# Two gated long convolutions: the filters' first transforms as 64-row products, and another layout of the accumulation banks

## The chip, the core and the metric

The kernel runs on one core of a Trainium2 chip. The metric is the time of one execution on the device, in microseconds. The kernel before takes 766.85 us (median of three runs, 766.52 to 771.82). Engines are named as in the profile: PE (matrix products, with its weight loads apart as PEld), DVE, ACT, POOL and SP, which issues most transfers.

## What is computed

x of 2048 positions and 512 channels passes through four layers: A, B, A, B, each added to x, each on a layer norm of x.

```python
def _A_ref(q, k, v, shift_k, ssm_k, ssm_D):      # q = layernorm(x)
    k_shift = sum over t < 4 of k_pad[:, t:t + S, :] * shift_k[:, 3 - t]
    kv = k_shift * v
    y = causal_conv_by_fft(kv, ssm_k)             # per channel, length 2048
    return q * (y + kv * ssm_D)

def _B_ref(u, log_A_real, A_imag, C_real, C_imag, log_dt, D_skip):   # u = layernorm(x)
    K = 2 * real(sum over 128 modes of C * dt * exp((-exp(log_A_real) + 1j * A_imag) * dt * pos))
    return causal_conv_by_fft(u, K) + u * D_skip
```

Layer A's convolution doesn't depend on x, so the kernel does it once and uses it twice. B's taps K are worked out from the modes.

## The kernel before, in words

A transform of length 4096 is done in two steps of matrix products. For channels in groups of 32, the first step (`fwd_group`, `fwd_rows`, line 171) multiplies a tile of 128 rows, which are two halves of 64 rows, each by its own weights. In the *whole* form (`full`) the weights `wz[:, a, :]` have 128 rows of which the other half are zeros, and 16 channels at a time give two products of 128x256 that share one PSUM bank. In the *half* form, for 32 channels at a time, each product takes 64 rows only, writes 512 columns, and the two of a pair (a = 1, 0) lie in the two banks of a double bank (`wide_bank`, tag "f1"). Either way two transposes on DVE (lines 191 and 189) bring 32 channels out of PSUM. The second step (`f2_chunk`, line 196) makes a chunk `pu` of four frequencies from all 128 channels of a quarter; a quarter has eight chunks.

PSUM has eight banks. Until the convolution of B begins they are: "c1", three, for everything of layer A (pf, pu, pi, po and acc); "pm", two, for the magnitudes of the tap stream and for the spectra of B; "pa", two, for its angles; "pk", one, for its sums. After that: "c1" four and "f1" two double banks. So the half form is used in the convolution of B alone.

The work until then is two generators, run in turns (`run_steps`: one step of the stream, two of the other):

- The stream (`taps`, lines 544 to 578) makes B's taps in 64 steps: `angles` (line 484: a product into pa, rounding on DVE, a second product into the same bank), `waves` (lines 495 to 497, sines on ACT), `products` (lines 507 to 511, POOL and DVE, the last readers of the bank pa) and `contract` (line 521 into pk). Every eighth step makes twelve `mags` (line 469 into pm, exponentials on ACT, line 475) for the next two groups of 8 channels at once. After each 16 steps a quarter of B's spectrum follows (`spectrum_quarter(1, ...)`, 12 steps, one with each step of the stream).
- The other (`diagonal`) makes the four quarters of A's spectrum (`spectrum_quarter(0, ...)`, 4 + 8 steps each: first transforms of the tile kk, then the chunks pu, which ACT copies into one of two buffers pc and SP writes to DRAM, lines 247 and 248), and in the same steps `gated`: POOL makes four products `term` (line 619), ACT copies the first into a bank `acc` (line 625), DVE adds the others (line 627) and multiplies into `un` (line 629), 16 groups in all. `un` uses the buffers of pc. Row statistics of x are also taken here (line 637). When all this has been issued, the convolution of A follows (lines 270 to 327).

Then come `gated_update` (lines 724 to 743: ut on ACT, x on DVE), the norm, and the convolution of B, whose tiles in SBUF take the place of the stream's. The order of instructions on each engine is the tile framework's, which lists what is ready by the order of the program, on a timeline that it works out when it builds the kernel.

Of the kernel before, what the change touches and what calls it, by code (L numbers as in the profile page):

```python
# [9 lines left out]
F32 = mybir.dt.float32  # L10
# [5 lines left out]
PSUM = bass.MemoryType.PSUM  # L16
# [83 lines left out]
def kernel(ctx: ExitStack, tc: tile.TileContext, out, x_in, kv_in, ssmk_in, ssmd_in,  # L100
                           la_in, ai_in, cr_in, ci_in, ldt_in, ldtb_in, dsk_in,
                           w1_in, w2_in, mm_in, w4_in, minus_in, tt_in, tg1_in, tg2_in, dbg=None):
    nc = tc.nc
    V, S, G, T = nc.vector, nc.scalar, nc.gpsimd, nc.tensor

    def sbuf(stack, name, side="left"):
        return stack.enter_context(tc.tile_pool(name=name, bufs=1, side=side, reuse_waits="tile"))
# [8 lines left out]
    kdram = [dram.tile([128, 512], F32, name=f"kdram{g}") for g in range(16)]  # L116
# [18 lines left out]
    wz = cpool.tile([128, 2, 128], F32, name="wz")  # L135
# [4 lines left out]
    st0 = cpool.tile([128, 16, 6], F32, name="st0")  # L140
    var, rs, nm, nb = [cpool.tile([128, 16], F32, name=n) for n in ("var", "rs", "nm", "nb")]

    psum, w1, swapped = {}, [], [None]

    def bank(name, tag="c1"):
        pool, bufs = psum[tag]
# [13 lines left out]
    def fwd_rows(src, pf, j, step, rows, full):  # L160
        for a in (1, 0):
            half = slice(0, 128) if full else slice(64 * a, 64 * a + 64)
            w = wz[:, a, :] if full else w1[0][half, :]
            rhs = src(half, j, step)[:, rows, :]
            o = pf[:, a].rearrange("p x t r -> p t x r")[:, rows]
            if len(rhs.shape) == 4:
                o = o.rearrange("p t (i x) r -> p t i x r", i=rhs.shape[2])
                rhs = rhs.rearrange("p t i (x r) -> p t i x r", r=2)
            else:
                rhs = rhs.rearrange("p t (x r) -> p t x r", r=2)  # L170
            yield T.matmul(o, w, rhs, start=True, stop=True)  # L171
# [51 lines left out]
    def spectrum_quarter(which, q, src, pool, zlast, zb, tag):  # L223
        z = pool.tile([128, 64, 32, 2], F32, name="zk", tag="z", bufs=zb) if which else z_of_a()
        dr = pool.tile([1, 128], F32, name="dr", tag="dr", bufs=1)
        nc.sync.dma_start(dr, (ssmd_in, dsk_in)[which][:, 128 * q:128 * q + 128])
        for g in range(4):
            kk = pool.tile([128, 512], F32, name="kk", tag="kk", bufs=3 - which)
            nc.sync.dma_start(kk, src[4 * q + g])
            d = dr[:, 32 * g:32 * g + 32]  # L230
            if which == 0:
                kv = kk.rearrange("p (t c) -> p t c", c=32)
                view = lambda ps_, j, n: kv[ps_, :, j:j + n]
            else:
                kv = kk.rearrange("p (i t c) -> p t i c", i=4, c=8)
                view = lambda ps_, j, n: kv[ps_, :, j // 8:(j + n) // 8, :]
                d = d.rearrange("p (i c) -> p i c", c=8)

            G.tensor_add(kv[0:1, 0], kv[0:1, 0], d)  # L239
            fwd_group(view, z, 32 * g, 32, 16, zlast[-zb] if len(zlast) >= zb else None, tag)  # L240
            yield
        for c in range(NCH):
            pu, ins = f2_chunk(z, c, None, tag)
            if c == NCH - 1:
                zlast.append(ins)
            pc = pool.tile([128, CK * 128], F32, name="pc", tag="pc", bufs=2)
            S.copy(pc, pu.rearrange("p k c -> p (k c)"))  # L247
            nc.sync.dma_start(spec[which][q][c], pc)
            yield
# [96 lines left out]
    for a in range(2):  # L346
        half = slice(64 * a, 64 * a + 64)
# [77 lines left out]

    pctx = ExitStack()
    pp = pctx.enter_context(tc.tile_pool(name="ps", bufs=1, space=PSUM, reuse_waits="tile"))
    NPA = 2
    NPM = 2
    psum["c1"] = (pp, 7 - NPA - NPM)  # L430
    psum["pm"] = (pp, NPM)

    for tag, bufs in (("c1", 7 - NPA - NPM), ("pa", NPA), ("pk", 1)):
        pp.tile([128, 512], F32, name=tag, tag=tag, bufs=bufs)
    wk = sbuf(gctx, "wk")
    kp = sbuf(gctx, "spec_k")
    NT = 3
# [26 lines left out]
    def mags(gi, k, col):  # L464
        h, s = divmod(k, 2)
        hs = slice(64 * h, 64 * h + 64)
        pm = pp.tile([128, 512], F32, name="pm", tag="pm", bufs=NPM)
        rhs = tabs["tg2"][hs] if col == 2 else tabs["tg1"][hs, 8 * s:8 * s + 8, :]
        mt = T.matmul(pm, rows[gi][hs, 1, :], rhs, start=True, stop=True)  # L469
        if col == 2:  # L470
            ms[gi, h] = wk.tile([128, 16, 96], F32, name="m", tag="m", bufs=NM)
            m = ms[gi, h][:, :, 64:96]
        else:
            m = ms[gi, h][:, 8 * s:8 * s + 8, 0:64]
        i = S.activation(m, pm.rearrange("p (c i) -> p c i", c=16 if col == 2 else 8), AF.Exp)  # L475
        if last_sin[0] is not None:
            after(i, last_sin[0])
        last_exp[0] = i
# [58 lines left out]
    zlast_k, todo = [], []  # L537
# [6 lines left out]
    def taps():  # L544
        load_rows(0)
        load_rows(1)

        def exps(gi):
            for k in range(4):
                if k % 2 == 0:  # L550
                    mags(gi, k, 2)
                mags(gi, k, 1)

        for n in range(64 + LP + LC):
            gi, k = divmod(n, 4)
            if n < 64:
                if k == 0:
                    if gi > 0 and gi < 15:
                        load_rows(gi + 1)
                    if EORD == 1:  # L560
                        exps(gi)
                    elif EORD == 3 and gi % 2 == 0:
                        exps(gi)
                        exps(gi + 1)
                if n == XN:
                    root = normalizer(0, 16, lambda t: st0[:, t, :])
                    after(root, last_exp[0])
                    last_exp[0] = root
                angles(gi, k)
                waves(gi, k)  # L570
            if 0 <= n - LP < 64:
                products(*divmod(n - LP, 4))
            m = n - LP - LC
            if 0 <= m < 64:
                contract(*divmod(m, 4))
                if m % 16 == 15:
                    todo.append(spectrum_quarter(1, m // 16, kdram, kp, zlast_k, 1, "pm"))
            yield

    def stream():  # L580
# [20 lines left out]
    with ExitStack() as actx:  # L601
        ap = sbuf(actx, "conv_a", "right")
        zlast = []
        ZA = 2
# [38 lines left out]
        def steps_a(q):  # L643
            z, us = {}, {}
            nop = lambda: None

            def load(g):
                us[g] = ap.tile([128, 16, 32], F32, name="u", tag="kk", bufs=3)
                nc.sync.dma_start(us[g].rearrange("p t c -> p (t c)"), kv_d[4 * q + g])

            def fwd(g):
                if g == 0:
                    z[0] = z_of_a()
                u = us[g]
                fwd_group(lambda ps_, j, n: u[ps_, :, j:j + n], z[0], 32 * g, 32, 16, zlast[4 + q - ZA])
                if g < 3:
                    load(g + 1)
            turns = [lambda g=g: fwd(g) for g in range(4)]
            if LAGA > 2:
                turns = [nop, turns[0], turns[1], lambda: (turns_last[0](), turns_last[1]())]  # L660
                turns_last = [lambda: fwd(2), lambda: fwd(3)]
            return (lambda: z[0]), [nop] * 7 + [lambda: load(0)] + [nop] * 4 + turns
# [6 lines left out]
        def diagonal():  # L669
# [17 lines left out]
                    yield  # L687
            for _ in kvs:
                yield
            yield from convolution(0, {"conv": ap}, steps_a, finish_a, lag=LAGA, ahead=AHA, nk=NKA, ns=NSA, nw=NWA, inplace=True,  # L690
                                   add_dve=ADA, zlast=zlast)

        RT = 1
        RD = 2
        diag = diagonal()
        for _ in range(4):
            next(diag)
# [2 lines left out]

    xp = sbuf(ctx, "xp", "right")
    st = xp.tile([128, 16, 4, 6], F32, name="st")
    w1.append(xp.tile([128, 128], F32, name="w1"))
    nc.sync.dma_start(w1[0], w1_in)
    st_all = lambda t: st[:, t, :, :].rearrange("p q s -> p (q s)")

    def gated_update(buffer, spare, rnd, load_x=False):
# [49 lines left out]
    EF = 1  # L757
# [25 lines left out]
    def steps_b(rnd, q):  # L783
        z = {}
        u = rotating("u", [128, 16, 128], "u", 3)
# [26 lines left out]
        early = {}  # L812
# [12 lines left out]
        def fwd(c):  # L825
            if c == 0:
                z[0] = rotating("zu", [128, 64, 32, 2], "zu", 2)
            if c % 2 == 0:
                fwd_group(src(c), z[0], 16 * c, 32, 32 if "f1" in psum else 16,
                          full="f1" not in psum or q == 0 and c < 2 * EF, early=early.get(c))  # L830
        return (lambda: z[0]), [lambda c=c: start(c) for c in range(NCH)] + [lambda c=c: fwd(c) for c in range(NCH)]

    def finish_b(rnd, q, g, po):
# [29 lines left out]
    for _ in range(2 * NCH):  # L863
        next(first)
    gctx.close()
    pctx.close()
    pp2 = ctx.enter_context(tc.tile_pool(name="ps2", bufs=1, space=PSUM, reuse_waits="tile"))
    psum["c1"] = (pp2, 4)
# [80 lines left out]
```

## Time and profile before

| | us |
|---|---|
| median of three runs | 766.85 |
| lowest, highest | 766.52, 771.82 |
| the profiled execution | 765.14 |
| its span in the profile | 763.3 |
| PE busy | 625.0 |
| DVE busy | 528.7 |
| ACT busy | 487.7 |
| POOL busy | 454.7 |
| mean granted clock of PE | 0.895 |

In rows of the profile, L171 is line 171 of the kernel, `pf<-kk,wz` says that tiles pf are written from kk and wz, `128*128 128x256` that a product has 128 rows and 128 columns of weights and an output of 128x256. One product of 32-bit numbers is two records. In a list of groups the busy time and the mean duration in ns stand first, then the idle time of the engine just before them and what ended it. In a timeline the first number is the start, the second the duration. A tile named x in the first part of the kernel is the half of x's memory that holds z, the result of the first step. The table of stretches gives each engine's busy time, then the granted clock (1.00 is full speed) and the DMA engines' busy share.

### The profile page before, as it was taken

How to read it: one execution, taken by the hardware profiler on the slowest of the kernel's cores; microseconds unless marked ns; L12 is line 12 of the kernel's file. 1: busy time of each engine (PE TensorE's matmuls, PEld its weight loads, DVE VectorE, ACT ScalarE, POOL GpSimd, SP SyncE). 2: the span in 40 equal slices, each digit the busy share in tenths (PEclk: the TensorE clock that was granted, in tenths of full speed). 3: DMA queues.
4: the chain of work that ended last, by engine and by line, in shares of the span. 5: the costliest groups of instructions: out<-in, count | busy, mean ns of one | idle time of the engine just before them, and what ended most of it. 6: DMA issues, size and time to landing. Idle time of an engine off the chain costs nothing.

```text
span 763.3 us, 14414 instructions
## 1 busy us (share of the span) xinstructions
PE 625.0 (82%) x5064; PEld 442.4 (58%) x5064; DVE 528.7 (69%) x961; ACT 487.7 (64%) x884; POOL 454.7 (60%) x473
## 2 busy tenths in 40 slices
PE   2387897788989989999989568499698935799996
PEld 1255565566667757767665345276566812476773
DVE  7855859689657586555747767216587899868775
ACT  4245485645686964975986997059655538668572
POOL 5855968855367864756854114208676811388693
PEclk9666979799999999999999569589999887899999
DMA  9666666667756645674747710257967431078782
GB/s 325 225 223 238 199 218 210 225 192 242 230 136 185 162 137 148 180 222 111 216 137 223 278 42 30 76 178 190 265 180 201 113 111 55 21 201 226 194 255 100
DMA packets 80396, 135.47 MB, mean 177 GB/s; under 512 B 8508, under 2 KB 29508, under 8 KB 78788
## 3 DMA queue, kind: packets, MB, share of 16 engines
q1 hardware_dynamic: 79428, 132.13, 57.9%
q0 software_dynamic: 896, 2.43, 1.1%
q8 instruction: 40, 0.66, 0.4%
q14 instruction: 32, 0.26, 0.1%
HBM read 98.87 MB, written 35.65 MB: 176 GB/s over the span
## 4 chain that ended last, share of the span: by engine, by line
PE 46%; DVE 13%; DMA 12%; ACT 12%; issue 10%; POOL 3%; SPq 2%; ACTq 0%; DVEq 0%; POOLq 0%
PE pu L196 14%; PE pf L171 12%; PE pi L293 7%; PE po L314 4%; DMA kab<-spec 3%; PE pk L521 3%; PE pm L469 3%; PE pa L484 2%; DMA ya_d<-ya 2%; PE pa L489 2%; DMA spec<-pc 2%; ACT m L475 1%; DMA xt<-x_in 1%; DMA rows_d<-hl 1%; DVE x L735 1%
## 5 line engine op out<-in xcount | busy, mean ns | idle before, releaser
L283 POOL TENSOR_TENSOR sw<-sw,kab 128x512 f32<-128x512 f32 x96 | 123.5, 1291 | 72.4 <-ACT sw L280 65.6
L281 DVE TENSOR_TENSOR vv<-pu,kab 128x512 f32<-128x512 f32 x96 | 65.0, 681 | 70.5 <-ACT sw L280 40.2
L171 PE MATMUL pf<-kk,wz 128*128 128x256 f32 x256 | 79.3, 452 | 40.7 <-POOL kk L239 38.2
L293 PE MATMUL pi<-vv,mm 128*128 128x128 f32 x768 | 107.5, 284 | 4.0 <-DVE vv L281 2.3
L507 POOL TENSOR_TENSOR xye<-co,m 128x512 f32<-128x512 f32 x64 | 75.4, 1178 | 57.3 <-issue 32.4
L293 PEld LDWEIGHTS pi<-vv,mm 128*128 128x128 f32 x768 | 96.3, 196 | 17.5 <-issue 11.4
L284 POOL TENSOR_TENSOR vv<-vv,sw 128x512 f32<-128x512 f32 x76 | 98.5, 1298 | 13.1 <-DVE vv L281 9.8
L619 POOL TENSOR_TENSOR term<-kvt 128x512 f32<-128x512 f32 x64 | 81.6, 1294 | 34.6 <-ACT acc L625 24.5
L279 ACT ACTIVATE sw<-pu 64x512 f32<-64x512 f32 x96 | 57.0, 594 | 65.1 <-PE pu L196 61.6
L196 PEld LDWEIGHTS pu<-zu,w 128*128 128x128 f32 x512 | 64.0, 194 | 40.5 <-DVE vv L281 15.0
L171 PEld LDWEIGHTS pf<-kk,wz 128*128 128x128 f32 x256 | 53.0, 221 | 57.3 <-POOL kk L239 40.2
L196 PE MATMUL pu<-x,w 128*128 128x128 f32 x512 | 77.6, 298 | 9.5 <-ACT pc L247 3.5
L196 PE MATMUL pu<-zu,w 128*128 128x128 f32 x512 | 73.6, 287 | 10.6 <-DVE vv L281 10.4
L196 PEld LDWEIGHTS pu<-x,w 128*128 128x128 f32 x512 | 69.2, 206 | 22.3 <-ACT pc L247 5.1
L247 ACT COPY pc<-pu 128x512 f32<-128x512 f32 x64 | 36.8, 588 | 58.5 <-PE pu L196 38.7
L475 ACT ACTIVATE m<-pm 128x512 f32<-128x512 f32 x96 | 54.1, 602 | 22.0 <-PE pm L469 20.7
L495 ACT ACTIVATE co<-pa 128x512 f32<-128x512 f32 x64 | 38.4, 601 | 40.5 <-PE pa L489 40.0
L508 DVE TENSOR_TENSOR xye<-pa,m 128x512 f32<-128x512 f32 x64 | 43.3, 677 | 22.7 <-ACT pa L496 19.3
L521 PE MATMUL pk<-xye 128*32 128x64 f32 x2048 | 52.2, 238 | 7.3 <-POOL xye L511 7.0
L314 PE MATMUL po<-w,w 128*64 128x512 f32 x192 | 53.3, 631 | 5.9 <-DVE w L308 5.5
L469 PE MATMUL pm<-tg,rw 64*128 64x512 f32 x96 | 45.6, 546 | 14.7 <-ACT m L475 12.2
L191 DVE STREAM_TRANSPOSE x<-pf 128x512 f32<-128x512 f32 x64 | 45.3, 709 | 17.6 <-PE pf L171 16.6
(137 smaller groups left out, 1205.3 us busy)
## 6 DMA issues: line engine op xcount, KB each, us to landing
kab<-spec SPq DMA_DIRECT2D x188, 256.0 KB, 4.1
spec<-pc SPq DMA_DIRECT2D x64, 256.0 KB, 3.1
kvt<-kv_in SPq DMA_DIRECT2D x16, 624.0 KB, 8.0
yaq<-ya_d SPq DMA_DIRECT2D x8, 1024.0 KB, 8.8
kk<-ssmk_in SPq DMA_DIRECT2D x16, 256.0 KB, 2.8
kv_d<-un SPq DMA_DIRECT2D x16, 256.0 KB, 3.5
kdram<-ks SPq DMA_DIRECT2D x64, 64.0 KB, 2.7
kk<-kdram SPq DMA_DIRECT2D x16, 256.0 KB, 2.6
```

Of the source, the lines that this page charges most:

```text
L171: yield T.matmul(o, w, rhs, start=True, stop=True)
L196: ins = T.matmul(pu[:, i, :], w2[:, c * CK + i, :], z[:, :, c * CK + i, :], start=True, stop=True)
L281: V.tensor_mul(vv, pu, kabs[s][:, 0])
L283: (V if last else G).tensor_mul(sw, sw, kabs[s][:, 1])
L284: (V if last or s % add_dve == add_dve - 1 else G).tensor_add(vv, vv, sw)
L293: i1s[t] = T.matmul(pi[:, i, :], mm[:, c * CK + i, :], vvs[t][:, i, :], start=True, stop=True)
L314: ins = T.matmul(po[64 * a:64 * a + 64], w4, ws[g][:, :, 16 * a:16 * a + 16, :].rearrange("p x t r -> p t x r"), start=True, stop=True, ti ...
L469: mt = T.matmul(pm, rows[gi][hs, 1, :], rhs, start=True, stop=True)
L475: i = S.activation(m, pm.rearrange("p (c i) -> p c i", c=16 if col == 2 else 8), AF.Exp)
L507: G.tensor_mul(xye[:, 0, :, 32:96], co[:, :, 1:65], m[:, :, 32:96])
L521: T.matmul(pk[32 * i4:32 * i4 + 32, 2 * k + i, :], xye[:, r, 4 * i + i4, 64:96], xye[:, r, 4 * i + i4, 0:64], start=r == 0, stop=r == 1, t ...
L619: G.tensor_mul(term, kvt[:, 3 - j:19 - j, :], tap(j))
```

## The change

Until the convolution of A begins, PSUM is laid out as "pa" three banks, "pk" one, "c1" two and "f1" one double bank. The magnitudes use "pa" together with the angles. Where "f1" exists, the first transforms of both filters' spectra are done in the half form, 32 channels at a time, with `wz[half, a, :]` as weights; those are the same numbers as in w1, whose tile and load go. When the convolution of A begins (`stage_banks(4, 0)`), the general banks and the double bank are given back and "c1" gets four; from there on the first transforms of B's remaining quarters and of the convolution are in the whole form, as before. B's spectra use "c1" in place of "pm". The condition on `rnd` in the last but one hunk leaves the first round as it was, since "f1" isn't there at that time.

```diff
-            w = wz[:, a, :] if full else w1[0][half, :]
+            w = wz[half, a, :]
...
-            fwd_group(view, z, 32 * g, 32, 16, zlast[-zb] if len(zlast) >= zb else None, tag)
+            fwd_group(view, z, 32 * g, 32, 32 if "f1" in psum else 16, zlast[-zb] if len(zlast) >= zb else None, full="f1" not in psum)
...
-    NPA = 2
-    NPM = 2
-    psum["c1"] = (pp, 7 - NPA - NPM)
-    psum["pm"] = (pp, NPM)
-
-    for tag, bufs in (("c1", 7 - NPA - NPM), ("pa", NPA), ("pk", 1)):
+    NPA = 3
+    NPC = 2
+    sctx = ExitStack()
+
+    def stage_banks(n, wide):
+        sctx.close()
+        pool = sctx.enter_context(tc.tile_pool(name=f"ps{n}{wide}", bufs=1, space=PSUM, reuse_waits="tile"))
+        psum["c1"] = (pool, n)
+        psum.pop("f1", None)
+        if wide:
+            psum["f1"] = (pool, wide)
+
+    for tag, bufs in (("pa", NPA), ("pk", 1)):
         pp.tile([128, 512], F32, name=tag, tag=tag, bufs=bufs)
+    stage_banks(NPC, 1)
...
-        pm = pp.tile([128, 512], F32, name="pm", tag="pm", bufs=NPM)
+        pm = pp.tile([128, 512], F32, name="pm", tag="pa", bufs=NPA)
...
-                    todo.append(spectrum_quarter(1, m // 16, kdram, kp, zlast_k, 1, "pm"))
+                    todo.append(spectrum_quarter(1, m // 16, kdram, kp, zlast_k, 1, "c1"))
...
-                fwd_group(lambda ps_, j, n: u[ps_, :, j:j + n], z[0], 32 * g, 32, 16, zlast[4 + q - ZA])
+                fwd_group(lambda ps_, j, n: u[ps_, :, j:j + n], z[0], 32 * g, 32, 32 if "f1" in psum else 16, zlast[4 + q - ZA], full="f1" not in psum)
...
+            stage_banks(4, 0)
             yield from convolution(0, {"conv": ap}, steps_a, finish_a, lag=LAGA, ahead=AHA, nk=NKA, ns=NSA, nw=NWA, inplace=True,
...
-    w1.append(xp.tile([128, 128], F32, name="w1"))
-    nc.sync.dma_start(w1[0], w1_in)
...
-                          full="f1" not in psum or q == 0 and c < 2 * EF, early=early.get(c))
+                          full="f1" not in psum or rnd == 1 and q == 0 and c < 2 * EF, early=early.get(c))
...
+    sctx.close()
     pctx.close()
```

More of the change, by code (lines that the diff above doesn't have):

```diff
@@ L141 @@
     var, rs, nm, nb = [cpool.tile([128, 16], F32, name=n) for n in ("var", "rs", "nm", "nb")]
-    psum, w1, swapped = {}, [], [None]
+    psum, swapped = {}, [None]
     def bank(name, tag="c1"):
```

## The prediction, made before the changed kernel ran

> **What bounds the kernel now.** I read the page first, then the table of busy time by stretch, for three stretches whose ends I took from the tiles: the gating of kv and the spectra of filter A (46 to 200 us), the convolution of A with the tap stream beside it (200 to 414), the end of the tap stream (414 to 511).
>
> ```profile
> span 763.3 us, 14414 instructions
> PE 625.0 (82%) x5064; PEld 442.4 (58%) x5064; DVE 528.7 (69%) x961; ACT 487.7 (64%) x884; POOL 454.7 (60%) x473
> ```
>
> ```profile
> core 0: us, PE busy (x) PEld busy (x) DVE busy (x) ACT busy (x) POOL busy (x), PEclk, DMA share, GB/s
> 46.00:200.00 154.00, 130.76 (x1210) 93.17 (x1210) 113.35 (x211) 90.22 (x158) 108.27 (x118) 0.84 0.68 217
> 200.00:414.00 214.00, 204.31 (x1938) 146.09 (x1927) 136.45 (x214) 159.74 (x277) 137.84 (x141) 0.98 0.59 166
> 414.00:511.00 97.00, 65.77 (x600) 47.01 (x600) 50.08 (x115) 61.34 (x120) 23.28 (x33) 0.72 0.37 127
> ```
>
> The average of 82% hides three cases. In the middle stretch PE works 204 of 214 us and nothing else matters much. In the last it works two thirds of the time, at a clock of 0.72, and waits for a chain through ACT, POOL and DMA. In the first, where nearly all of the change lies, PE is busiest (85%), but DVE (74%) and POOL (70%) are close behind. So there I need the chain of waits, cut to that stretch:
>
> ```profile
> by line: PE pu L196 12.1%; PE pf L171 11.4%; PE pm L469 9.0%; issue 8.2%; DMA xt<-x_in 7.3%; DMA spec<-pc 6.0%; PE pk L521 5.0%; PE pa L489 3.5%; ACT pc L247 2.9%; DVE st L637 2.9%; ACT pa L496 2.8%; PE pa L484 2.7%; DVE xye L508 2.5%; DVE
> ```
>
> PE holds 12.1 + 11.4 + 9.0 + 5.0 + 3.5 + 2.7 = 44% of the chain; the products that the change halves (pf) hold 11.4% of 154 us, 17.6 us. The rest of their time lies beside DVE, ACT and DMA work.
>
> **The first transforms.** Groups of instructions from 46 to 200 us, then two rows of the timeline, the old form in the convolution of A and the new one as the convolution of B already has it, both at full clock:
>
> ```profile
> L171 PE MATMUL pf<-kk,wz 128*128 128x256 f32 x128 | 35.9, 417 | 0.6 <-issue 0.4
> L191 DVE STREAM_TRANSPOSE zk<-pf 128x512 f32<-128x512 f32 x8 | 5.5, 690 | 0.0
> ```
>
> ```profile
> 289.42 1.99 PE L171 MATMUL pf<-u,wz 128*128 128x256 f32 x8
> 520.18 1.99 PE L171 MATMUL pf<-u,w 64*128 64x512 f32 x8
> ```
>
> A product is two records, and a group of 32 channels takes four products before: the 128 records are 16 groups at 2.24 us. Twelve are A's, four are the first quarter of B (eight zk transposes, two to a group). B's other twelve groups come after the step that lays the banks out anew and stay as they are, as do all of the convolutions'. In the new form a group is two products, four records, so the second row holds two groups and the first one: 1.0 against 2.0 us. The 16 groups fall from 35.9 to about 18 us. What lies on the chain falls by half: **-8.8 us**. The other 9 us are saved beside other work; some of it becomes chain when PE is next late, and I take **-2** (0 to -9).
>
> Four more groups of A run before 46 us, and there I take 0, because the stream can't start before its rows come back from DRAM:
>
> ```profile
> 29.58 10.14 DMA rows_d<-hl
> 39.74 5.40 DMA raw<-rows_d
> 46.60 0.78 PE pm L469 x2
> ```
>
> The transposes out of the bank stay two to a group. Those of the wide form in B:
>
> ```profile
> L189 DVE STREAM_TRANSPOSE zu<-pf 128x512 f32<-128x512 f32 x56 | 36.0, 687 | 18.0 <-PE pf L171 18.0
> ```
>
> 687 against 690 ns: nothing. But the wide bank is single. The next pair waits for both transposes of the last, 1.0 + 2 x 0.69 = 2.4 us a group, which is no shorter than the 2.24 before. It costs nothing as long as PE has the stream's and the second transforms' products to do meanwhile, which holds on the stretches where pf is on the chain; without that cover the gain is gone (a rival below). The Trainium skill, TensorEngine Tiling (Array Packing), section PSUM Bottleneck, says the same as a rule: tiling speeds TensorE up but not the emptying of PSUM. By that rule alone the sum would hold no gain from these products; the trace of B agrees in so far as DVE's rows don't get shorter.
>
> **Two banks in place of three for pu and acc.** pf leaves the shared banks, but one of them goes too. An acc is long in its bank; the shortest and the longest of 14 holds in the stretch, from the copy to the end of un:
>
> ```profile
> 98.55 0.61 ACT L625 COPY acc<-term 128x512 f32<-128x512 f32 x1
> 171.90 0.59 ACT L625 COPY acc<-term 128x512 f32<-128x512 f32 x1 [5.75 <-DVE un L629]
> ```
>
> ```profile
> 102.36 0.69 DVE L629 TENSOR_TENSOR un<-acc,kvt 128x512 f32<-128x512 f32 x1 [0.79 <-ACT co L495]
> 185.69 0.67 DVE L629 TENSOR_TENSOR un<-acc,kvt 128x512 f32<-128x512 f32 x1
> ```
>
> 4.5 and 14.5 us; 14 holds at some 9 us are 126 us of 154, so for 0.82 of the time one of the two banks is taken and pu has a single one. Then PE's eight records (1.1 us) and ACT's copy take turns.
>
> ```profile
> L196 PE MATMUL pu<-x,w 128*128 128x128 f32 x224 | 37.5, 323 | 8.0 <-ACT pc L247 3.2 <-DVE un L629 2.7 <-DVE x L191 1.9
> L196 PE MATMUL pu<-zk,w 128*128 128x128 f32 x32 | 4.3, 279 | 0.0
> L247 ACT COPY pc<-pu 128x512 f32<-128x512 f32 x32 | 18.2, 591 | 19.0 <-DMA spec<-pc 11.2 <-PE pu L196 6.7 <-DMA kv_d<-un 1.0
> ```
>
> 224 + 32 records are 32 chunks. The exposed part of a turn is the copy and two hand-overs, about 0.75 us: 32 x 0.75 x 0.82 = 20 us at most, of which 5.9 (3.2 + 2.7) are there today. At least it is 0, since the copies already wait 11.2 us for their own buffers, which nothing here changes. Behind a pu that waits for a bank, the whole of PE's queue stands, the stream's products with it. But the order of PE's instructions is planned with this wait in view, and other products can be put into it. I take **+4** (0 to +14).
>
> **acc no longer behind pf.** Of the waits from 46 to 200 us, and of the groups up to 46 us:
>
> ```profile
> POOL term L619 <- ACT acc L625: 24.5, 7, 5.6
> ACT acc L625 <- DVE x L191: 4.0, 3, 1.5
> ```
>
> ```profile
> L625 ACT COPY acc<-term 128x512 f32<-128x512 f32 x3 | 1.8, 586 | 11.9 <-DVE x L191 11.9
> ```
>
> acc waited 4.0 us, and 11.9 before 46 us, for a transpose to free a bank of the first transforms. Those are now apart, so POOL's terms, which wait 24.5 us for acc, can start earlier by a group (four terms of 1.3 us) at 46. **-4** (0 to -12: half of the 24.5).
>
> **The clock.** Over the three stretches PE is busy 85, 95 and 68% and the clock is 0.84, 0.98 and 0.72: 0.007 for each per cent. With 18 us less work in about 147 us, PE is busy 77% (130.8 - 18 = 113) and the clock falls to about 0.79. PE's other 113 us then cost 113 x (0.84/0.79 - 1) = 7 us, of which its 44% of the chain is **+3** (0 to +7). The Trainium skill, TensorE: Matmul & The Clock Gate, part 1, gives a sharper rule: the clock halves after an idle window of some 3.4 us. By it the term would be near 0 and the sum 3 us less, as the longest idle gap of PE in the first stretch is this one of 3.9 us:
>
> ```profile
> 66.43 0.79 PE L484 MATMUL pa<-tt,rw 64*128 64x512 f32 x1 [3.90 <-ACT pa L496]
> ```
>
> **Angles and magnitudes share three banks; B's spectra use the general ones.** In the convolution of A there were 3 + 2 + 2 banks and are now 4 + 3, for the same products, on a PE that is busy 95%. 0 (-4 to +4: at most half of the 10 idle us of that stretch either way). In the last stretch the two banks for the magnitudes are seen to hold ACT up:
>
> ```profile
> 429.75 1.28 PE L469 MATMUL pm<-tg,rw 64*128 64x512 f32 x2 [3.23 <-ACT m L475]
> 433.16 1.28 PE L469 MATMUL pm<-tg,rw 64*128 64x512 f32 x2 [2.13 <-ACT m L475]
> ```
>
> ```profile
> 428.64 0.57 ACT L495 ACTIVATE co<-pa 128x512 f32<-128x512 f32 x1
> 429.12 1.06 ACT L475 ACTIVATE m<-pm 128x512 f32<-128x512 f32 x2
> 430.07 2.55 ACT L724 ACTIVATE ut<-yaq,rs 128x512 f32<-128x512 f32 x4
> 432.52 1.07 ACT L475 ACTIVATE m<-pm 128x512 f32<-128x512 f32 x2
> ```
>
> Two magnitudes, then four ut (2.55 us), again and again, because only two fit. With three, one or two of these turns go and the stream's sines start 2.5 to 5 us earlier. On the other side, angles are made ready meanwhile in banks of their own (co<-pa at 428.64), and now they come after. The ut still have to be done, but the stream's end is what the B convolution waits for. **-3** (-5 to +4).
>
> The load of w1 (64 KB) goes, and the same weights are read from wz: 0, it was one load, made once.
>
> **Sum.** -8.8 - 2 + 4 - 4 + 3 + 0 - 3 = -10.8. The profiled execution took 765.14 us, so 754.3. The median of the runs is 766.85, 1.7 above it; on that scale **756.0**. About 1% either way (7.7 us) is what a measurement tells from no change.
>
> **The rivals.**
> *The emptying bounds.* If the first transforms are paced by the single wide bank (2.4 us a group against 2.24), the saved products only leave PE idle: the -8.8, -2 and -3 go, the +4 and the acc's -4 cancel, the clock's +3 is hardly felt: 765 to 768, say 766. For it: DVE at 74% and a chain that is PE for 44% alone. Against: the chain rests on pf itself, and only while there is something else for PE does the single bank bind.
> *Two banks starve pu.* The +14 instead of +4, the clock's +7, no gain at acc because acc now waits for a pu: -8.8 + 14 + 7 = +12, so 779. It decides as soon as more than 0.35 us per chunk (9 of the 26 us that 32 chunks x 0.82 make at 1 us) is exposed. For it: acc holds one bank 82% of the time. Against: in the trace the copies wait for transfers of pc more (11.2) than PE waits for banks (5.9).
> *The gating runs free.* If POOL's terms set the pace, the -4 becomes -12 and the pf saving off the chain counts in full (-9 for -2): 756 - 8 - 7 = 741. For it: the 24.5 us, and an acc in its bank 82% of the time. Against: POOL is busy only 70%.
>
> **Chances.** The forecast 0.50, the emptying 0.20, starving 0.20, free gating 0.10. Faster by over 1% (under 759.2): 0.42 of the forecast's 0.50, and all of the free gating, 0.52. Within 1%: the forecast's other 0.08 and 0.18 of the emptying, 0.26. Slower: 0.02 of the emptying and the starving, 0.22. The range runs from 740, under the free gating, to 777, which leaves out half of the starving. The forecast's own is 748 to 763.
>
> **What would show it.** The first product of the A convolution stands at 198 us now:
>
> ```profile
> 198.06 1.13 PE L171 MATMUL pf<-u,wz 128*128 128x256 f32 x4
> ```
>
> I expect it near 189. Further: pf out of kk as 80 records of 64x512 and 96 of 128x256, the former at about 0.28 us each in the stretch (1.1 us a group); acc's waits for a transpose gone, and PE's waits for the copy pc and for un above 5.9 us by less than 5; the clock from 46 us on near 0.79; the magnitudes in turns of three. Wrong if the A convolution starts no earlier than 196, if PE waits over 15 us for banks of pu, if the gain arises after 200 us, or if the stretch from the end of the A convolution to the B convolution, 97 us now, grows.

## The result and the profile after

The changed kernel takes 742.79 us (median of four runs, 741.31 to 749.53) beside 766.68 of the kernel before in the same comparison (four runs): a ratio of 0.9707, 95% interval 0.9616 to 0.9798. That is 24 us less, where 10.8 were forecast. The profiled execution took 741.69 us. Of the kernels further below, e1_split, e2_whole and e10_swap were profiled in an execution slower than their others, so their moments lie somewhat late, and the ratios don't rest on them. From the page of the changed kernel, the lines that answer to those of before:

```profile
span 739.6 us, 14284 instructions
PE 596.3 (81%) x4984; PEld 412.2 (56%) x4984; DVE 533.1 (72%) x961; ACT 486.4 (66%) x882; POOL 456.3 (62%) x473
```

PE's share is what it was (81% for 82%), with 29 us less busy time in a span 24 us shorter: here the share tells nothing of the gain. The stages do. Three moments cut the span: the first product of A's convolution, the last of its copies `ya`, and the first second-transform product of B's convolution. Busy time of each engine in these stretches, before and then after:

```profile
core 0: us, PE busy (x) PEld busy (x) DVE busy (x) ACT busy (x) POOL busy (x), PEclk, DMA share, GB/s
46.00:198.10 152.10, 128.86 (x1174) 91.90 (x1174) 111.85 (x208) 89.53 (x158) 106.42 (x116) 0.84 0.67 215
198.10:413.70 215.60, 205.91 (x1958) 147.06 (x1957) 137.95 (x217) 160.18 (x278) 139.39 (x143) 0.98 0.59 168
413.70:508.30 94.60, 63.37 (x584) 45.49 (x585) 49.58 (x114) 59.99 (x117) 23.58 (x33) 0.71 0.37 125
```

```profile
46.00:204.90 158.90, 127.43 (x1229) 81.90 (x1227) 116.95 (x212) 98.99 (x173) 110.18 (x118) 0.85 0.68 223
204.90:431.20 226.30, 205.22 (x2161) 145.81 (x2160) 150.95 (x241) 175.47 (x304) 152.90 (x156) 0.98 0.53 149
431.20:490.40 59.20, 41.21 (x277) 34.62 (x275) 36.04 (x86) 40.51 (x90) 8.32 (x16) 0.88 0.64 220
```

The first stretch is 6.8 us longer, the second 10.7 longer, and the third 35.4 shorter; B's part after it is 5.8 us shorter (255.0 to 249.2). Together -23.7. What had changed inside them shows best in the products of the stream's sums, pk, cut by the same three moments (the first stretch from 0; the columns are the stretch, its length, the busy time on PE, PEld and DVE, and then clock and transfers as above), before and then after:

```profile
0.00:198.10 198.10, 17.95 (x704) 13.67 (x704) 5.48 (x10) 0.84 0.71 230
198.10:413.70 215.60, 24.46 (x960) 16.71 (x960) 9.02 (x16) 0.98 0.59 168
413.70:508.30 94.60, 9.81 (x384) 7.42 (x384) 3.29 (x6) 0.71 0.37 125
```

```profile
0.00:204.90 204.90, 18.20 (x768) 13.44 (x768) 6.68 (x12) 0.88 0.71 236
204.90:431.20 226.30, 28.73 (x1216) 20.43 (x1216) 10.04 (x18) 0.98 0.53 149
431.20:490.40 59.20, 1.27 (x64) 0.98 (x64) 1.08 (x2) 0.88 0.64 220
```

Before, 384 of the 2048 products (twelve of the stream's 64 steps, at 32 each) came after the end of A's convolution; now 64 do. The time saved on PE wasn't used to start A's convolution earlier. PE's last product for A's spectra (pu out of x) ends at 192.6 us, where it ended at 197.5 before; but A's first pf follows it after 12.3 us and not after 0.6, and in these 12.3 us the timeline shows no gap of PE, which works for the stream alone (pk, pm and pu out of zk):

```profile
191.44 1.16 PE L196 MATMUL pu<-x,w 128*128 128x128 f32 x8
204.86 1.46 PE L171 MATMUL pf<-u,wz 128*128 128x256 f32 x6
```

So the last stretch, where the stream had run with PE two thirds busy at a clock of 0.71, is nearly empty of its sums, and of the angles and magnitudes that feed them. What is left of the stream there is B's spectrum, 181 records of pf and pu for 136 before.

The ends of the two strands are seen in three rows, one for each kind of instruction with its first and last start. Before, then after:

```profile
L521 PE MATMUL pk<-xye x2048: 216/219/317, 72.8 to 484.4; 128*32 128x64 f32 x187
L666 ACT COPY ya<-po x16: 565/586/634, 275.4 to 413.7; 128x512 f32<-128x512 f32 x16
L196 PE MATMUL pu<-zu,w x512: 269/272/580, 508.3 to 744.9; 128*128 128x128 f32 x171
```

```profile
L529 PE MATMUL pk<-xye x2048: 216/219/317, 75.6 to 434.9; 128*32 128x64 f32 x187
L674 ACT COPY ya<-po x16: 580/587/609, 285.0 to 431.2; 128x512 f32<-128x512 f32 x16
L196 PE MATMUL pu<-zu,w x512: 270/272/421, 490.4 to 721.1; 128*128 128x128 f32 x171
```

Call S the last pk, A the last ya and B the first pu out of zu. Before, B followed S by 23.9 us, and A had been over for 94.6. The chain of waits that leads into B ran then through the last quarter of B's spectrum, the tail of the stream:

```profile
491.92 3.79 PE pf L171 x8
...
496.51 5.14 PE pu L196 x24
...
502.33 2.30 DMA spec<-pc
```

After, B follows A by 59.2 us, and S by 55.5. In the chain after A's end stands what these 59 us are made of:

```profile
431.18 0.59 ACT ya L674
431.78 3.63 DMA ya_d<-ya
435.48 6.57 DMA yaq<-ya_d
442.08 0.73 ACT ut L731
...
464.74 3.14 DMA kk<-kdram
...
470.83 3.85 ACT u L804 x10
...
476.41 2.06 DMA spec<-pc
...
481.51 0.59 ACT pc L247
...
482.15 7.46 PE pf L171 x32
```

Ten us to DRAM and back, the gated update, the norm, the first transforms: a path that waited behind the stream before and is now on the chain itself. It isn't alone there. From 464.74 (the rows kk of B's last quarter) to the copy pc at 481.51 the chain goes through B's spectrum again, whose copies share ACT with the gated update; the first transforms of B's convolution start only behind it. So the 59 us are a distance read from profiles, in which the tail of the stream still has a part.

### The profile page after: what moved, and what is told of

It reads as the page before. It is cut to its first block, busy times and chain, and to the rows that moved or that the text cites. A ratio compares the mean times of both kernels' runs of the same rounds, so it can differ in the third digit from the quotient of the medians.

```text
span 739.6 us, 14284 instructions
## 1 busy us (share of the span) xinstructions
PE 596.3 (81%) x4984; PEld 412.2 (56%) x4984; DVE 533.1 (72%) x961; ACT 486.4 (66%) x882; POOL 456.3 (62%) x473
## 4 chain that ended last, share of the span: by engine, by line
PE 46%; DVE 17%; DMA 12%; ACT 11%; issue 7%; POOL 5%; SPq 1%; DVEq 0%; POOLq 0%; ACTq 0%
PE pu L196 14%; PE pf L171 12%; PE pi L293 8%; PE po L314 4%; PE pm L477 3%; PE pk L529 3%; DVE x L742 2%; DMA kk<-kdram 2%; DMA kab<-spec 2%; DMA kdram<-ks 2%; POOL term L627 1%; PE pa L492 1%; DMA spec<-pc 1%; ACT co L505 1%; ACT co L503 1%
## 5 line engine op out<-in xcount | busy, mean ns | idle before, releaser
L293 PE MATMUL pi<-vv,mm 128*128 128x128 f32 x768 | 105.9, 282 | 3.3 <-POOL vv L284 2.2
L284 POOL TENSOR_TENSOR vv<-vv,sw 128x512 f32<-128x512 f32 x76 | 98.3, 1298 | 12.3 <-DVE vv L281 9.8
L293 PEld LDWEIGHTS pi<-vv,mm 128*128 128x128 f32 x768 | 94.8, 194 | 16.9 <-issue 8.4
L171 PE MATMUL pf<-kk,wz 128*128 128x256 f32 (+1 forms) x176 | 65.0, 627 | 47.0 <-issue 17.7
L627 POOL TENSOR_TENSOR term<-kvt 128x512 f32<-128x512 f32 x64 | 81.9, 1296 | 23.5 <-ACT acc L633 10.7
L196 PE MATMUL pu<-x,w 128*128 128x128 f32 x512 | 81.2, 306 | 8.7 <-ACT pc L247 5.4
L196 PEld LDWEIGHTS pu<-x,w 128*128 128x128 f32 x512 | 72.1, 213 | 25.9 <-ACT pc L247 7.5
L171 PE MATMUL pf<-u,wz 128*128 128x256 f32 (+2 forms) x280 | 78.4, 497 | 6.5 <-DVE zu L189 3.9
L196 PE MATMUL pu<-zu,w 128*128 128x128 f32 x512 | 72.1, 283 | 8.1 <-DVE vv L281 7.1
L171 PEld LDWEIGHTS pf<-kk,wz 128*128 128x128 f32 (+1 forms) x176 | 29.7, 224 | 63.7 <-issue 32.6
L280 ACT COPY sw<-pu 64x512 f32<-64x512 f32 x96 | 55.5, 578 | 1.1
L171 PEld LDWEIGHTS pf<-u,wz 128*128 128x128 f32 (+1 forms) x280 | 41.2, 193 | 24.0 <-issue 12.7
```

Of the source, the lines that this page charges most:

```text
L196: ins = T.matmul(pu[:, i, :], w2[:, c * CK + i, :], z[:, :, c * CK + i, :], start=True, stop=True)
L280: swapped[0] = S.copy(sw[64:128], pu[0:64])
L284: (V if last or s % add_dve == add_dve - 1 else G).tensor_add(vv, vv, sw)
L293: i1s[t] = T.matmul(pi[:, i, :], mm[:, c * CK + i, :], vvs[t][:, i, :], start=True, stop=True)
L627: G.tensor_mul(term, kvt[:, 3 - j:19 - j, :], tap(j))
```

## The experiments

Two theories. By the first, **the balance** (theory M in the texts recorded before each run), the gain is that the two strands end together: B starts at the later of S + 24 to 32 and A + 54 to 61, before had S 71 us behind A, and whatever moves work from the one to the other gives the same. These distances were read from the profiles below as they came in. By the second, **the saved work** (theory H), it is the PE time that the half form frees. A rival to both is **the plan's accident** (theory L): any edit makes the framework order the instructions anew. What the recorded texts call theory S is that the three shared banks let the stream run ahead. All runs first, the moments from their profiles in us, the ratio to the kernel before on the same chip with its 95% interval:

| kernel | A's first pf | A | S | B | ratio |
|---|---|---|---|---|---|
| before | 198.1 | 413.7 | 484.4 | 508.3 | 1 |
| after | 204.9 | 431.2 | 434.9 | 490.4 | 0.9707 (0.9616 to 0.9798) |
| e4_w1 | 196.8 | 411.5 | 484.2 | 508.9 | 1.0025 (0.9973 to 1.0077) |
| e1_split | 227.2 | 463.9 | 564.7 | 593.7 | 1.0972 (1.0876 to 1.1068) |
| e3_pa2 | 216.0 | 442.8 | 536.6 | 563.9 | 1.0671 (1.0604 to 1.0738) |
| e2_whole | 232.4 | 429.9 | 484.5 | 516.5 | 0.9945 (0.9895 to 0.9994) |
| e5_before_23 | 201.2 | 423.8 | 461.8 | 489.4 | 0.9751 (0.9637 to 0.9864) |
| e6_after_49 | 192.8 | 405.3 | 469.9 | 497.8 | 0.9735 (0.9662 to 0.9808) |
| e7_after_47 | 224.0 | 432.4 | 446.1 | 491.4 | 0.9632 (0.9560 to 0.9705) |
| e11_whole_23 | 240.3 | 455.2 | 424.9 | 508.9 | 0.9928 (0.9876 to 0.9979) |
| e8_only_a | 208.4 | 425.0 | 431.2 | 485.5 | 0.9521 (0.9452 to 0.9590) |
| e9_only_a_817 | 201.2 | 408.8 | 459.2 | 489.1 | 0.9650 (0.9582 to 0.9719) |
| e10_swap | 208.7 | 449.3 | 453.1 | 507.6 | 0.9777 (0.9671 to 0.9883) |
| e12_only_a_swap | 202.8 | 418.3 | 438.1 | 479.1 | 0.9550 (0.9486 to 0.9614) |

**e4_w1: the kernel before without the load of w1.**

```diff
-            w = wz[:, a, :] if full else w1[0][half, :]
+            w = wz[half, a, :]
...
-    w1.append(xp.tile([128, 128], F32, name="w1"))
-    nc.sync.dma_start(w1[0], w1_in)
```

> The kernel before, with only the tile w1 and its load gone and the half-form weights read from wz. All theories of a cause in the banks or the products: 765 to 768 us, no change. If the plan of the instructions reacts to any small change by many us (theory L, luck of the plan), more than 5 us either way.

1.0025: the load was worth nothing, as forecast. It speaks against the plan's accident too, as far as one small edit can: S, A and B came out within 2.2 us of the kernel before.

**e1_split: the half form, but angles and magnitudes apart**, two banks and one, the rest as after.

```diff
-    NPA = 3
+    NPA = 2
+    NPM = 1
...
-        pm = pp.tile([128, 512], F32, name="pm", tag="pa", bufs=NPA)
+        pm = pp.tile([128, 512], F32, name="pm", tag="pm", bufs=NPM)
```

> The changed kernel, but angles keep two banks of their own and magnitudes one (2 + 1 in place of three shared). Theory H (the half-form products free TensorE before 200 us, and the plan gives the time to the tap stream): as the changed kernel, 739 to 748 us, the stream's last product pk near 435 us. Theory S (the three shared banks let the stream run ahead): the gain goes for the most part, 757 to 768 us, last pk at 465 us or later.

**e3_pa2: angles and magnitudes share two banks**, and pu and acc have three again (five in A's convolution).

```diff
-    NPA = 3
-    NPC = 2
+    NPA = 2
+    NPC = 3
...
-            stage_banks(4, 0)
+            stage_banks(5, 0)
```

> The changed kernel, but angles and magnitudes share two banks and the general banks are three (five in the convolution of A). Theory S: the stream falls back, 757 to 775 us. Theory H: 739 to 750 us. If two general banks starve the second transforms and acc, as my prediction priced at 4 us, the waits of TensorE for pc and un from 46 to 200 us fall from 7.4 us to about 3.

9.7% and 6.7% slower than before: medians of 844.59 and 819.41 us, far above what either theory expected. The saved products are the same in both, so without three shared banks the double bank costs far more than it gives: the stream ends 80 and 52 us later. ACT's waits from 46 to 560 us for the two kinds of product, first e1_split, then e3_pa2, then after:

```profile
ACT m L484 <- PE pm L478: 55.9, 45, 3.8
ACT co L504 <- PE pa L498: 49.7, 27, 5.2
```

```profile
ACT co L503 <- PE pa L497: 62.8, 27, 7.8
ACT m L483 <- PE pm L477: 21.6, 23, 4.1
```

```profile
ACT co L503 <- PE pa L497: 31.2, 19, 3.8
ACT m L483 <- PE pm L477: 16.2, 18, 3.4
```

(us, times, the longest.) Before, with two and two, they were 40.0 and 20.7. One bank alone for the magnitudes lets ACT wait 45 times; with three in common it waits less than with four apart. e3_pa2 also gives the price of two banks for pu and acc, which the prediction had put at +4. PE's waits for the copy pc and for un from 46 to 200 us are 0.7 and 0.5 us with three banks (e3_pa2); with two (after) they are:

```profile
PE pu L196 <- ACT pc L247: 5.4, 4, 1.6
PE pu L196 <- DVE un L637: 2.0, 3, 1.1
```

1.2 against 7.4, where about 3 had been expected; before had 5.9.

**e2_whole: the new banks without the half form.** pu, acc and the first transforms share four banks throughout.

```diff
-    stage_banks(NPC, 1)
+    stage_banks(4, 0)
```

> The new bank layout without the half form: angles and magnitudes share three, the general banks are four from the beginning, all first transforms in the whole form. Theory H: no gain, 760 to 768 us, last pk at 465 us or later. Theory S: most of the gain, 743 to 752 us, last pk near 440 us. If both halves add, 750 to 758.

0.9945: the layout by itself gives about half a per cent. With the same banks for the stream the half form, with its double bank, is then worth 0.9945 - 0.9707 = 2.4%. This alone would say "the saved work". But S and A differ too, 484 and 430 against 435 and 431, so it had to be asked what balance does without the half form.

**e5_before_23: the kernel before, with two steps of the stream to three of the other**, in place of one to two. No product is saved and no bank moved.

```diff
-        run_steps([(stream(), RT), (diag, RD)])
+        taps_ = stream()
+        run_steps([(taps_, 1), (diag, 2), (taps_, 1), (diag, 1)])
```

> The kernel before with its banks, but the stream gets two steps to three of the other generator, in place of two to four. Theory M (the B convolution begins at the later of two ends, the stream's last product plus 25 us and the last copy ya of the A convolution plus 59 us): the stream ends earlier than 484 us, the A convolution later than 414, and the time falls to 745 to 757 us. If the stream's pace before is set by its own two and two banks and not by the order of the program: the stream ends at 475 us or later, and 764 to 785 us.

0.9751. One edit that only shifts the turns gives most of what the whole change gives (0.9707), and the two intervals overlap; its own runs from 0.9637 to 0.9864, so it is a gain, of a size that is loosely known. S comes 22.6 us earlier, A 10.1 later, and B 18.9 earlier, as the balance says.

**e6_after_49, e7_after_47 and e11_whole_23: the balance moved elsewhere.** After with four steps of the stream to nine of the other:

```diff
-        run_steps([(stream(), RT), (diag, RD)])
+        taps_ = stream()
+        run_steps([(taps_, 1), (diag, 2)] * 3 + [(taps_, 1), (diag, 3)])
```

> The changed kernel with a slower stream, four steps to nine in place of four to eight. There the A convolution's end (431 us) is what the B convolution waits for, and the stream has some 30 us to spare. Theory M: the A convolution ends near 422 us, the stream's last product near 445, and the time falls by 5 to 9 us, to 733 to 738. If the plan doesn't follow the order of the program: 740 to 755.

After with four to seven:

```diff
-        run_steps([(stream(), RT), (diag, RD)])
+        taps_ = stream()
+        run_steps([(taps_, 1), (diag, 2)] * 3 + [(taps_, 1), (diag, 1)])
```

> The changed kernel with a faster stream, four steps to seven in place of four to eight. Theory M: the A convolution ends at 438 us or later, and the time rises to 748 to 757. If the stream's end still counted: 735 to 742.

And e2_whole with the two to three of e5_before_23, by the same lines:

> The new bank layout in the whole form, with the stream at two steps to three. It separates the half form from the balance of the two ends. If the half form's worth is TensorE's time (20 groups at about 1.1 us, 22 us) on top of balanced ends: the B convolution from 500 to 508 us, time 750 to 760. If balance was all of the gain: 735 to 745. If the layout in the whole form is worse for other reasons: 765 and more.

The rule for B fits all three: e6_after_49 is bound by S again (469.9 + 27.9), the other two by A (432.4 + 59.0, 455.2 + 53.7). The times were not those expected. e6_after_49 was to be 5 to 9 us faster than after and is no faster (0.9735 for 0.9707); e7_after_47 was to be slower and isn't (0.9632): its time is that of its other outcome, in which the stream's end still counts, though B came 45.3 us after S and 59.0 after A; e11_whole_23 lies just above its 750 to 760. How far a step moves the ends was guessed badly, and in e7_after_47 even the direction: with a faster stream S came 11.2 us later than in after, and A 1.2. The steps set the order of the program, and the plan decides what comes of it.

e11_whole_23 is no clean test, since it went past the balance (S 30 us ahead of A) where e2_whole fell short of it (S 55 us behind A). The balanced case can be read between the two, though. On the straight line from e2_whole to e11_whole_23, S + 28 falls from 512 to 453 and A + 57 rises from 487 to 512; they meet at about 495. With the same 28 and 57, the line from before through e5_before_23 and a little beyond meets at about 484, and that between after and e6_after_49 at about 477. These are estimates from two points each. By them the new layout without the half form loses about 11 us against the old one at equal balance, the half form wins about 18 in it, and the change as a whole about 7. The old kernel lay 24 us off its own balance (508 - 484) and after lies 13 off (490 - 477). So of the 18 us by which B starts earlier, the lines put about 11 down to balance and 7 to less work. That division isn't shown: the distances of 28 and 57 are known to some 4 us, e2_whole's moments lie late, and e7_after_47 doesn't lie on the line of its kernel. The best ratios measured in each, 0.9751 for the old products and banks and 0.9632 for the new, are 1.2% or 9 us apart, but their intervals overlap.

The next run separates more. It has the new banks and most of the half form, and in the same comparison as e5_before_23 its interval (0.9452 to 0.9590) lies clear below that one's (0.9637 to 0.9864). By the line above, e5_before_23 had some 5 us left to its balance (489 - 484), 0.7%, which would bring it to about 0.968, an estimate that is still above e8_only_a's interval. So balance is a large part of the gain, and most likely not all of it; no run of the old kernel at its own balance settles it.

**e8_only_a: the half form for A's spectrum alone**, B's first quarter in the whole form.

```diff
+            wide = "f1" in psum and not which
-            fwd_group(view, z, 32 * g, 32, 32 if "f1" in psum else 16, zlast[-zb] if len(zlast) >= zb else None, full="f1" not in psum)
+            fwd_group(view, z, 32 * g, 32, 32 if wide else 16, zlast[-zb] if len(zlast) >= zb else None, full=not wide)
```

> The changed kernel with the half form for the spectra of A alone; the four groups of B's first quarter stay whole, in the two general banks. Theory H by TensorE's time: a fifth of the half form's gain goes (4 of 20 groups), 745 to 750 us. If it is the freed banks and the plan more than the products: 755 us or more.

0.9521: neither of the two expected times, but faster than both. Its interval is clear of after's (not of that of e7_after_47), with sixteen records more on PE (5000 for 4984). The profiles show 5.0 us of the difference (spans of 734.6 and 739.6), 4.9 of it before B.

**e9_only_a_817: e8_only_a with eight to seventeen turns**, to take the last us out of A's path.

```diff
-        run_steps([(stream(), RT), (diag, RD)])
+        taps_ = stream()
+        run_steps([(taps_, 1), (diag, 2)] * 7 + [(taps_, 1), (diag, 3)])
```

> The half form for the spectra of A alone, and a slightly slower stream (eight steps to seventeen in place of eight to sixteen). Theory M (the B convolution begins at the later of the stream's last product plus 24 to 32 us and the last ya plus 59 to 61 us): with the half form for A alone the second is 25 us the later, so a slower stream moves both together: last ya near 418 us, last pk near 445, the B convolution from about 478, time 725 to 732 us. If the plan doesn't follow so small a step: 730 to 742.

It overshot: S 459.2 where 445 was expected, A 408.8 for 418, and B is bound by S. One step more of the other strand in every 24 moved S by 28 us; at 0.9650 the kernel is no faster than e8_only_a.

**e10_swap and e12_only_a_swap: the two products of a pair in the other order**, in after and in e8_only_a. No work changes; how far does a new plan alone move the time?

```diff
-        for a in (1, 0):
+        for a in (0, 1):
```

> The changed kernel with the two products of each first transform in the other order (a = 0 before a = 1), in the whole form too; nothing is added or taken away. It measures theory L, how much the time depends on the plan alone: under 4 us either way, 739 to 747, if the causes found so far are all; 8 us and more if the plan's details count as much as they.

> The half form for the spectra of A alone, with the two products of each first transform in the other order. If keeping B's first quarter whole is better for a reason of its own, this stays clearly under the changed kernel's ratio to the kernel before (0.971): 0.95 to 0.96, 730 to 740 us. If that advantage was the plan's luck: 0.965 to 0.98, 743 to 755 us. The rule of the two ends holds in either case: the B convolution begins at the later of last pk plus 24 to 32 us and last ya plus 54 to 61.

+0.7% for after and +0.3% for e8_only_a, both within their intervals. The first is about 5 us, between the two outcomes that had been named, so an accident of the plan of this size isn't excluded. But the kernel with A alone in the half form is the faster one in both orders, by 1.9% and by 2.3% (0.9777 to 0.9550), with intervals that lie apart in both. So the advantage is more than this accident, as far as two orders can tell. In e12_only_a_swap the rule for B, recorded with its full ranges before the run, holds: B at 479.1, A + 60.8. What makes e8_only_a faster isn't settled. In after the wide bank is shared by A's groups and B's, and its products wait for both strands; groups from 46 to 200 us:

```profile
L171 PE MATMUL pf<-kk,wz 64*128 64x512 f32 x62 | 28.5, 814 | 12.5 <-issue 6.1 <-DMA kk<-kdram 3.3 <-DVE x L189 2.6
```

3.3 us of that are for B's rows from DRAM, and A's groups stand behind them in the bank. But the long casts on DVE (last section) sum to 21.0 us in after and to 16.8 in e8_only_a, and no run separates the two. Of all kernels here e8_only_a has the lowest ratio; e12_only_a_swap (0.9550) can't be told from it.

## Why the prediction was right or wrong

The sign and the range held, and the mechanism didn't: two of its four conditions for "wrong" came true. A's convolution starts at 204.9, not near 189 and later than the 196 named, and the gain arises after 200 us. That the time lies in the range is luck. The forecast's own band was 748 to 763; 742.79 lies below it, beside the 741 of the rival "the gating runs free", whose mechanism, POOL's terms setting the pace of the first stretch, wasn't what happened either: A's convolution began later, not earlier.

- **First transforms, -8.8 and -2.** The records are those forecast, 80 of 64x512 and 96 of 128x256. The time isn't: 62 records from 46 to 200 us take 28.5 us, not about 18, at 814 ns each, for a price taken from a pair of eight at full clock in B. In that stretch the wide products overlap others of 64 rows and run at 0.84. PE's busy time there fell by 8 us, not 18, and with more work in it: 768 records of pk for 736, 43 of pm for 37, 279 of pu for 256. The row of after that answers to the prediction's first stretch (130.76 before):

```profile
46.00:200.00 154.00, 122.53 (x1200) 78.09 (x1197) 115.83 (x210) 95.95 (x168) 109.94 (x117) 0.84 0.69 225
```

  **The failed step is that the chain's share of pf (11.4% of 154 us, halved) would come off that stretch.** PE's queue holds both strands, and the PE time that came free there went to the stream: the 12.3 us of its products that stand between the end of A's spectra and A's first pf.
- **The last stretch, -3.** It held the gain: 94.6 to 59.2 us. The prediction priced the banks in it (turns of magnitudes) and took the work in it as given. But the work there was what was left of the stream, and how much is left is set by all the PE time before it. Its own sentence, "the stream's end is what the B convolution waits for", was right, and could have told where freed time counts.
- **A's convolution, 0.** +10.7 us at the same PE work (205.2 for 205.9): PE's idle time grew from 9.7 to 21.1 us, and 203 more records lie in it, 256 more of pk among them.
- **Two banks for pu and acc, +4.** Waits 5.9 to 7.4 us, +1.5, within the size given. The starving at 779 us didn't come about.
- **acc, -4.** The waits for a transpose are gone; acc waits 1.2 us for un and 0.5 for a term. POOL's term, which waited 24.5 us for the copy, now waits 7.5 for it and 9.2 for DVE's acc, and the last un is issued at 187.7 for 194.3. The step holds in kind, with a last un 6.6 us earlier, and didn't bring A's convolution forward either.
- **Clock, +3.** It stayed 0.84 in that row, with PE busy 80% for 85%; the prediction's 0.007 for each per cent had 0.80 for that. The three stretches didn't lie on a line to begin with: 0.007 between the last and the first, 0.014 between the first and the second. And other kernels here show 0.77 (e7_after_47) and 0.89 (e11_whole_23) in the same stretch, with PE busy 127.1 and 133.8 of 154 us. The rule of the Trainium skill, TensorE: Matmul & The Clock Gate, part 1, by which the clock halves after an idle window of some 3.4 us, would have left the term near 0, as measured. But the trace doesn't bear out its reason. In after the granted clock is 0.52 from 162 to 170 us (eight records of pu take 2.07 us there, for 1.16 at 191), and the longest gap of PE in the ten us before was 0.52 us:

```profile
160.46 0.49 PE L477 MATMUL pm<-tg,rw 64*128 64x512 f32 x1 [0.17 <-ACT m L483]
161.47 1.77 PE L492 MATMUL pa<-tt,rw 64*128 64x512 f32 x3 [0.52 <-ACT m L483]
163.17 2.07 PE L196 MATMUL pu<-x,w 128*128 128x128 f32 x8
```

  What lowered it there isn't shown. Over the whole execution the clock rose from 0.895 to 0.933; of the three stretches in the tables of the result the last rose most, from 0.71 to 0.88.
- **w1, 0.** As measured alone.

Of the rivals, none was this one. "The emptying bounds" would have held the sum at 766, and the Trainium skill's rule behind it (TensorEngine Tiling (Array Packing), section PSUM Bottleneck) is seen in the 2.6 us that the wide products wait for a transpose of A's rows and in 0.4 for one of B's. What stays open: the 5.8 us after B's start (e4_w1, with B's start 0.6 us from before's, differs there by 3.4 us by itself, so some of it may be scatter), how the gain divides into balance and saved work, and the cause of e8_only_a.

## What to carry to other kernels

Where two strands share an engine and a third part waits for both, write down first by how much each end is late: here the time saved in the shared engine counted at the later end, far behind the place where it was saved. Before changing products or banks, shift the turns of the strands by a step and look at both ends; here that alone gave 0.9751. And a bank has a price in each strand, read off by moving one bank at a time: the same saved products made the kernel 7 to 10% slower until the two kinds of the stream's products shared three banks.

## What was unexpected in the hardware

A cast of 128x256 on DVE takes from 0.27 to 6.24 us in one execution. Two of them, and POOL's instructions at the time of the second, from the timeline of after:

```profile
315.43 0.28 DVE L470 CAST rw<-raw 128x256 fp32r<-128x256 f32 x1
327.10 6.24 DVE L470 CAST rw<-raw 128x256 fp32r<-128x256 f32 x1
```

```profile
327.02 0.71 POOL L519 TENSOR_TENSOR xye<-co,m 128x256 f32<-128x256 f32 x1
327.67 2.53 POOL L283 TENSOR_TENSOR sw<-sw,kab 128x512 f32<-128x512 f32 x2
330.13 1.21 POOL L515 TENSOR_TENSOR xye<-co,m 128x512 f32<-128x512 f32 x1
331.26 0.72 POOL L519 TENSOR_TENSOR xye<-co,m 128x256 f32<-128x256 f32 x1
331.89 1.30 POOL L284 TENSOR_TENSOR vv<-vv,sw 128x512 f32<-128x512 f32 x1
```

The cast began 0.08 us after POOL's first and ended 0.15 us after POOL's last, six instructions later. PE's next product of A's convolution stood 6.4 us behind DVE, at 335.25 us.

The Trainium skill, SBUF — State Buffer, section Who interferes with whom, says that a cast can take the port pair which DVE shares with GpSimd, and that the one who comes second is blocked for the other's whole instruction. The times agree with the block: a cast that begins well inside a running POOL instruction ends about 0.15 us after the end of one. How many it sits through differs. The cast at 123.91 (5.00 us) ended 0.15 us after POOL had finished the last of five in a row, like the one above; seven of the sixteen casts in after sat through one alone, though the next followed at once, as here:

```profile
370.72 0.59 DVE L470 CAST rw<-raw 128x256 fp32r<-128x256 f32 x1
```

```profile
370.46 0.69 POOL L519 TENSOR_TENSOR xye<-co,m 128x256 f32<-128x256 f32 x1
371.11 1.24 POOL L515 TENSOR_TENSOR xye<-co,m 128x512 f32<-128x512 f32 x1
```

What decides between the two isn't shown. The sixteen casts together take 21.0 us in after and 9.6 in e12_only_a_swap. No run took POOL's work away from beside them, so the cause is argued from the times.
